# Softmax steps, products with v, pair loads and token steps moved to other points of a hand-written order

## The chip, the cores and the metric

The kernel runs on one core of one Trainium2 chip. The metric is device time in microseconds: the median of three runs of the kernel before is 1833.87 us (1829.96 to 1837.31). A profile is one more execution, with its own time.

## What is computed

Pooled attention followed by two feed-forward layers. The queries are used as they are; keys and values are averaged over groups of 8 tokens first, so each head has 72 keys.

```python
batch, n_heads, seq, head_dim = (8, 8, 576, 64)
k_p = k.reshape(B, H, Sp, pool, D).mean(axis=3)      # pool = 8, Sp = 72
v_p = v.reshape(B, H, Sp, pool, D).mean(axis=3)
scores = scale * np.matmul(q, k_p.transpose(0, 1, 3, 2))
scores = scores - np.max(scores, axis=-1, keepdims=True)
attn = np.exp(scores)
attn = attn / (np.sum(attn, axis=-1, keepdims=True) + 1e-09)
x = np.matmul(attn, v_p)                             # then (B * S, H * D) = 4608 x 512
h = x @ w_in; y = np.maximum(0.01 * h, h) @ w_out    # d_ff = 2048
xn = y / sqrt(mean(y * y) + 1e-6) * rms_g
g = xn @ w_gate; out = (g * sigmoid(g) * (xn @ w_val)) @ w_out2   # d_ff = 1536
```

All is float32. The kernel splits each operand of a product into a high and a low part and adds three products of them, so each matrix product is three matmuls (`TERMS`).

## The kernel before

Each engine works off its own queue in order: at the end the kernel ties every instruction of an engine to the one emitted before it. The order in which the program emits is therefore the order in which each engine runs, and an instruction that waits holds up what is behind it on its engine. SP issues all DMAs, also in order.

**First layer, tiles j = 0 to 4.** The 4608 tokens are nine tiles of 512. For the first five, `h_half` computes half of an h chunk (six matmuls of 512 columns) and `y_unit` half of its contribution to y (six more), two chunks of f later. After the second half of h, ScalarE applies the leaky ReLU twice (`h_high`, L101) and VectorE subtracts (`h_low`, L620). Each such piece of six matmuls is a chunk, and after each chunk `attention_point()` runs what has been put on the next point: the late attention (`late_attention`) and the conversion of weights for later (side units).

**Late attention.** Attention of batches 0 and 1 stands in the list `FIRST`. Batches 2 to 7 are 30 query tiles (five a batch), and tile i starts at point s = 33 + 8 (i - 10); `after` is the start of the next tile. `stage(kind, b, t, points)` puts one step of a generator on each of the points:

- `s` (step_s): scores of the first four heads on TensorE (sc, L322), then maximum and subtraction on VectorE (L335, L336); the same for the other four heads; the exponential on ScalarE (L341); sum, small addition, reciprocal and multiplication on VectorE (L343 to L346). Six steps.
- `r`: copies on ScalarE (er, L374), at s + 5. `t`: transposition of the next tile's queries (qt) with its copy, at s + 5.
- `x` and `y`: transpositions of the softmax (xt, L383, and xr) with their evictions to at and atr, at s + 6 and s + 7.
- `kt`: transposed pooled keys of the next batch and their copies on ScalarE (L294), at s + 3 of the fourth and fifth tile of a batch.
- `av0`, `av1`: the products with v (L426, L431) for the first two and the last three query tiles, four each (p = 0 to 3, two heads each), at points of the tile that follows, with an eviction on ScalarE (L445 or L453) and, where x stays on the chip, a subtraction on VectorE (L460). Where x goes to DRAM, SP's store is put two points later.

On one point, stages that were put by an earlier tile come first. For batches 1 to 7 the scores, kt, qt, xt, xr and the products share two banks of PSUM (tag `att`).

**First layer, pairs.** The last four tiles of tokens are two pairs, computed with seven products in place of eight (`Quad`; p1 to p7 with the names x, y, w for its sums). While the second half of pair 0's output runs as pieces of six matmuls (`queue_out`, `out_part`, each second one issuing a load of w_out by `load_o`), the loop at L1639 also issues the four loads of pair 1's tokens (`pair_loads`: xst from x in DRAM), its token steps (`token_steps`: sums, and splits into high and low parts on ScalarE, VectorE and POOL) and the splits of pair 0's own second half (`second_half`, k = 4 to 15). `tick()` runs the side units. Four pieces are left for the next pair. The loads write the slots of `up` that second_half k = 0 to 7 have read.

**Second layer.** Five pairs with a gate, a value and an output product; not touched by the change, though the loop is shared (`kinds[q] == 1` marks pairs of the first layer; only at q = 0 is the next pair of that kind too).

The functions that the change touches and what calls them:

Of the kernel before, what the change touches and what calls it, by code (L numbers as in the profile page):

```python
# [23 lines left out]
def pooled_attention_then_two_ffns(  # L24
# [14 lines left out]
    B, H, S, D = q.shape  # L39
# [431 lines left out]
    def go(kind, b, t):  # L471
        if (kind, b, t) not in running:
            running[kind, b, t] = emit[kind](b, t)
        if running[kind, b, t] is not None:
            next(running[kind, b, t], None)
# [33 lines left out]
    def late_attention():  # L509

        def put(point, f):
            at_point.setdefault(point, []).append(f)

        def stage(kind, b, t, points):
            for point in points:
                put(point, lambda: go(kind, b, t))
            if kind in use:
                def free():
                    live["q" if kind == "t" else "kv"] -= 1
                put(points[0] + 3, free)  # L520

        start = {}
        for i in range(FIRST_LATE, len(tiles) + 1):
            start[i] = 33 + 8 * (i - 10)
        for r, point in enumerate((4, 9, 14, 28, 30)):
            stage("kp", 2, r, (point,))
        stage("kt", 2, 0, (28,) * 2)
        stage("kt", 2, 1, (32,) * 2)
        stage("t", 2, 0, (28,) * 2)
        for i in range(FIRST_LATE, len(tiles)):  # L530
            b, t = tiles[i]
            s, after = start[i], start[i + 1]
            stage("s", b, t, (s, s, s + 1, s + 1, s + 3, s + 4))
            stage("r", b, t, (s + 5,))
            stage("x", b, t, (s + 6,) * 3)
            stage("y", b, t, (s + 7,) * 3)
            if i + 1 < len(tiles):
                stage("t", *tiles[i + 1], (s + 5,) * 2)
            if t < 2:
                for k in range(3):  # L540
                    stage("vp", b, 3 * t + k, (s + 2 * k,) * 2 + (s + 2 * k + 2,) * 2)
            if t in (2, 3) and b + 1 < B:
                for k in range(3 if t == 2 else 2):
                    stage("kp", b + 1, 3 * (t - 2) + k, (s + 4 * (t - 2) + 2 * k,))
                stage("kt", b + 1, t - 2, (after + 3,) * 2)
            if t in (1, 4):
                for p in range(NP):
                    stage(f"av{t // 4}", b, p, (after + 1 + p,) * 3)

    point_now = [0]  # L550
    first_left = {"V1l5", "T14c"}
# [395 lines left out]
    pairs, kinds = [], []  # L947
# [207 lines left out]
    def load_a():  # L1155
        if a_count[0] < len(a_todo):
            i = a_count[0]
            a_count[0] += 1
            if len(a_todo[i]) == 3:
                load_o_into(a_todo[i], "a", i)  # L1160
                return
            q, p, m, s = a_todo[i]
            assert {f"{m}{p}_{c}" for c in range(2)} <= ready
            t = slot("a", i, f"a{m}{q}_{p}_{s}")
            if m == "h" and s in (0, 3):
                n = 512 if s == 0 else 256
                nc.sync.dma_start(
                    out=t.rearrange("p h n -> p (h n)")[:, :2 * n].rearrange("p (h n) -> p h n", h=2).bitcast(F32),
                    in_=wi_dram[2 * p + s // 3][:, :, 512 - n:],
                )  # L1170
                a_tiles[q, p, m, s] = t.rearrange("p h n -> p (h n)")[:, :2 * n].rearrange(
                    "p (h a c n) -> p a c h n", h=2, c=2, n=P
                )
                return
            k = 2 if s < 3 else 1
            nc.sync.dma_start(
                out=t.rearrange("p h n -> p (h n)")[:, :k * 512].bitcast(F32),
                in_=op_dram[m, p][:, s, 0:k].rearrange("p a c n -> p (a c n)"),
            )
            a_tiles[q, p, m, s] = t.rearrange("p h n -> p (h n)").rearrange(  # L1180
                "p (a c h n) -> p a c h n", a=2, c=2, h=2
            )
# [143 lines left out]
    def second_half(q, k):  # L1326

        f = blocks(q, 1)[k]
        src = up[q, "f", f // 2][:, f % 2, :]
        if k % 4 != 1:  # L1330
            t = per.tile([P, 2, N], F32R, tag="ghl", bufs=3, name=f"ug{q}_{f}")
        else:
            t = p2.tile([P, 2, N], F32R, tag="ahl", bufs=1, name=f"ug{q}_{f}")
        split(nc.scalar, t[:, HI, :], nc.gpsimd if k % 2 else nc.vector, t[:, LO, :], src)
        up[q, 2, f] = t
# [186 lines left out]
    def piece():  # L1522
        if pieces:
            pieces.pop(0)()
# [16 lines left out]
    def tick():  # L1541
        for x in late_side.pop(0) if late_side else ():
            x()

    for q, (_, n) in enumerate(pairs):
        assert not late_side or kinds[q] == 1
        quads = [Quad(q, p, m) for p, m in QUADS[kinds[q]]]
        more = q + 1 < len(pairs)
        loads, xs, norm = [], None, []
        if more:  # L1550
            xs, steps = (pair_loads if kinds[q + 1] == 1 else norm_steps)(q + 1)
            if kinds[q + 1] == 1:
                loads = steps
            else:
                norm = steps
        n_norm = len(norm)

        def between():
            if norm and (i >= 2 or i == 1 and len(norm) > n_norm - 2):
                norm.pop(0)()  # L1560

        def h_quad(i, a):
            def spot():
                if norm and (i >= 3 or i >= 1 and len(norm) > n_norm - 2):
                    norm.pop(0)()
                tick()

            def out_piece():
                piece()
                spot()  # L1570

            a.p1()
            spot()
            a.p6()
            spot()
            out_piece()
            a.p2()
            load_a()
            spot()
            a.p7()  # L1580
            spot()
            out_piece()
            a.p5()
            spot()
            a.p4()
            load_a()
            spot()
            out_piece()
            a.p3()
            load_a()  # L1590
            load_a()
            spot()
            out_piece()
            if q == i == 0:
                piece()
            queue_out(q, 0, (2 * a.p, 2 * a.p + 1))

        def quad(i, a):
            for step in (a.p6, a.p5, a.p2, a.p7):
                step()  # L1600
                between()
                if step == a.p2:
                    load_a()
                    load_a()
            piece()
            if i + 1 < len(quads):
                quads[i + 1].p1()
            a.p4()
            a.p3()
            load_a()  # L1610
            load_a()

            if i + 1 < (len(quads) if more else len(quads) - 2):
                piece()
            if a.m == "v":
                queue_out(q, 0, (2 * a.p, 2 * a.p + 1))

        for i, a in enumerate(quads):
            if kinds[q] == 1:
                h_quad(i, a)  # L1620
                continue
            if i == 0:
                a.p1()
            quad(i, a)
        assert not norm
        early, late = token_steps(q + 1, xs, kinds[q] == 1) if more else ([], [])
        if kinds[q] == 1:
            second_half(q, 0)
            second_half(q, 1)
            for i in range(4):  # L1630
                piece()
                tick()
                if i > 1:
                    second_half(q, i)
        while pieces:
            piece()
        queue_out(q, 1, blocks(q, 1))

        for i in range(len(pieces) - (4 if more else 0)):  # L1639
            if kinds[q] == 1:  # L1640
                if loads and i in (6, 9, 12, 15):
                    loads.pop(0)()
                piece()
                if early + late and (i >= 16 if kinds[q + 1] == 1 else i >= 4 and i % 2 == 0):
                    (early or late).pop(0)()
                for k in (4, 5) if i == 3 else (i // 2 + 4,) if i % 2 and i > 3 else ():
                    if k < F1:
                        second_half(q, k)
                tick()
                continue  # L1650
            if i % 3 == 0 and early + late:
                (early or late).pop(0)()
            piece()
        assert not early + late
# [41 lines left out]
```

## Time and profile before

| | |
|---|---|
| median of three runs | 1833.87 us |
| profiled execution, its own time | 1832.07 us |
| span of its instructions | 1830.4 us |
| TensorE (PE) busy | 1750.5 us, 96% |
| VectorE (DVE), ScalarE (ACT), GpSimd (POOL) busy | 934.7, 718.1, 649.1 us |
| mean granted clock of TensorE | 0.988 |
| DMA | 406.36 MB, mean 222 GB/s |

The profile names instructions by line, engine, operation and tile (out<-in). PE is TensorE's matmuls, PEld its weight loads, SPq the queue of SP. "Idle before" is the time in which an engine stood idle just before an instruction, with what ended it. The granted clock is a share of full speed: 1.0 is 2.4 GHz, 0.5 is 1.2 GHz. Late attention lies between about 170 and 645 us of the span, the two pairs of the first layer between 645 and 960 us, the second layer behind them.

### The profile page before, as it was taken

The page shows a single profiled execution, that of the slowest core. Times are in us where ns is not written, and L with a number is a line of the kernel's source. Part 1 is how long each engine was busy: PE and PEld are TensorE (multiplying, and loading weights), DVE is VectorE, ACT ScalarE, POOL GpSimd, SP SyncE. Part 2 cuts the span into 40 slices and gives each one's busy share as a digit, 9 for nine tenths or more (in the row PEclk, how much of TensorE's full clock was granted, in tenths as well). Part 3 has the DMA queues.
Part 4 walks back from the last instruction along what each step waited for, and adds up shares of the span by engine and source line. Part 5 has one row for each costly group of instructions (what it writes and reads, how often), then busy time and mean ns, then how long its engine had stood idle before and what let it go on. Part 6 is the DMA issues. An engine that isn't in the chain of part 4 may idle for free.

```text
span 1830.4 us, 24096 instructions
## 1 busy us (share of the span) xinstructions
PE 1750.5 (96%) x8440; PEld 1478.9 (81%) x8440; DVE 934.7 (51%) x1633; ACT 718.1 (39%) x1527; POOL 649.1 (35%) x797
## 2 busy tenths in 40 slices
PE   5899999999998999998999999999999999999999
PEld 4789777777777788876888888899788889988887
DVE  7984445545455544465665344445534444463331
ACT  5664344434444444444554333233233323322220
POOL 5632324545243013354534432045143304513330
PEclk9899999999999999998999999999999999999999
DMA  8543554545576469987987755687765668675562
GB/s 245 197 140 125 212 192 145 164 139 179 169 226 200 145 227 335 320 329 276 344 304 225 247 182 198 218 322 252 249 240 191 203 217 311 243 274 201 196 207 92
DMA packets 214729, 406.36 MB, mean 222 GB/s; under 512 B 58704, under 2 KB 116560, under 8 KB 214096
## 3 DMA queue, kind: packets, MB, share of 16 engines
q1 hardware_dynamic: 214608, 404.82, 65.4%
q8 instruction: 67, 1.10, 0.2%
q14 instruction: 54, 0.44, 0.1%
HBM read 328.21 MB, written 76.55 MB: 221 GB/s over the span
## 4 chain that ended last, share of the span: by engine, by line
PE 80%; DVE 9%; ACT 4%; DMA 3%; issue 2%; POOL 1%; SPq 1%; ACTq 0%; POOLq 0%; DVEq 0%
PE o L1364 15%; PE h L597 9%; PE o L1344 7%; PE y L642 7%; PE yg L1236 6%; PE yv L1236 6%; PE xg L1236 4%; PE xv L1236 4%; PE wg L1236 4%; PE wv L1236 4%; PE yh L1236 3%; PE wh L1236 2%; PE xh L1236 2%; PE sc L322 2%; DMA wo<-wo 1%
## 5 line engine op out<-in xcount | busy, mean ns | idle before, releaser
L1364 PE MATMUL o<-wo,u 128*128 128x512 f32 x1296 | 316.4, 392 | 3.3 <-DMA wo<-wo 3.2
L1364 PEld LDWEIGHTS o<-wo,u 128*128 128x128 f32 x1296 | 243.3, 189 | 52.8 <-DMA wo<-wo 4.2
L597 PE MATMUL h<-xhl,w_i 128*128 128x512 f32 (+1 forms) x996 | 253.5, 396 | 6.3 <-DVE ghl L620 5.0
L597 PEld LDWEIGHTS h<-xhl,w_i 128*128 128x128 f32 x996 | 177.7, 191 | 37.3 <-DVE ghl L620 5.4
L642 PE MATMUL y<-ghl,w_o 128*128 128x256 f32 (+1 forms) x768 | 154.6, 346 | 0.0
L98 POOL TENSOR_TENSOR u<-e2g,u 128x512 fp32r<-128x512 f32 (+1 forms) x25 | 29.6, 1182 | 311.8 <-ACT u L95 311.8
L620 DVE TENSOR_TENSOR ghl<-h,ghl 128x512 fp32r<-128x512 f32 (+1 forms) x83 | 55.7, 671 | 164.3 <-ACT h L101 164.1
L642 PEld LDWEIGHTS y<-ghl,w_o 128*128 128x128 f32 x768 | 118.1, 192 | 12.8
L642 PE MATMUL y<-ghl,wr 128*128 128x512 f32 x384 | 104.2, 407 | 0.0
L1344 PE MATMUL o<-u,wo 128*128 128x512 f32 x384 | 96.2, 389 | 0.0
L1344 PE MATMUL o<-ug,wo 128*128 128x512 f32 x384 | 89.6, 390 | 0.7 <-DMA wo<-wo 0.7
L1344 PEld LDWEIGHTS o<-ug,wo 128*128 128x128 f32 x384 | 72.0, 188 | 16.9 <-issue 1.9
L1344 PEld LDWEIGHTS o<-u,wo 128*128 128x128 f32 x384 | 72.1, 188 | 15.0
L1236 PE MATMUL yg<-T,ag 128*128 128x512 f32 (+1 forms) x360 | 84.0, 368 | 0.0
L1236 PE MATMUL yv<-T,av 128*128 128x512 f32 (+1 forms) x360 | 83.8, 368 | 0.0
L1236 PE MATMUL xg<-xa,ag 128*128 128x512 f32 (+1 forms) x360 | 83.7, 367 | 0.0
L1236 PE MATMUL xv<-xa,av 128*128 128x512 f32 (+1 forms) x360 | 83.7, 367 | 0.0
L642 PEld LDWEIGHTS y<-ghl,wr 128*128 128x128 f32 x384 | 69.5, 191 | 12.3
L1236 PEld LDWEIGHTS yg<-T,ag 128*128 128x128 f32 x360 | 66.0, 188 | 10.0 <-DVE e1v L1213 0.6
L1236 PEld LDWEIGHTS yv<-T,av 128*128 128x128 f32 x360 | 66.2, 188 | 9.5
L1236 PEld LDWEIGHTS xv<-xa,av 128*128 128x128 f32 x360 | 66.1, 188 | 9.6
L1236 PEld LDWEIGHTS xg<-xa,ag 128*128 128x128 f32 x360 | 66.1, 188 | 9.4
(204 smaller groups left out, 3424.1 us busy)
## 6 DMA issues: line engine op xcount, KB each, us to landing
wo<-wo SPq DMA_DIRECT2D x172, 512.0 KB
ag<-op_g SPq DMA_DIRECT2D x90, 512.0 KB
av<-op_v SPq DMA_DIRECT2D x90, 512.0 KB
wr<-wo SPq DMA_DIRECT2D x32, 512.0 KB
ah<-op_h SPq DMA_DIRECT2D x32, 512.0 KB
k<-in_k_dram SPq DMA_DIRECT2D x40, 256.0 KB
q<-in_q_dram SPq DMA_DIRECT2D x40, 256.0 KB
op_g<-parts_g SPq DMA_DIRECT2D x36, 256.0 KB
```

Source lines behind the costliest of these rows:

```text
L98: lo_eng.tensor_tensor(out=lo, in0=src, in1=hi.bitcast(F32), op=ALU.subtract)
L322: nc.tensor.matmul(pt[:, i * n:(i + 1) * n], y[:, p, :], kblk[b % 2][:, p * n:(p + 1) * n], start=True, stop=True,)
L597: nc.tensor.matmul(pt, w[:, sp, c * P:(c + 1) * P], x[c][:, mp, c0:c1], start=c == 0 and i == 0, stop=c == KC - 1 and i == 2,)
L620: nc.vector.tensor_tensor(out=t[:, LO, :], in0=pt, in1=t[:, HI, :].bitcast(F32), op=ALU.subtract)
L642: nc.tensor.matmul(pt, w[:, sp, m * P:(m + 1) * P], g[:, mp, a - c0:a - c0 + n], start=ydone[j, a] == 1 and i == 0 and m % per_bank == 0, ...
L1236: nc.tensor.matmul(pt, wt[:, a, c, sp, :], xt[:, mp, :], start=start and c == 0 and i == 0, stop=c == 1 and i == 2, skip_group_check=not s ...
L1344: nc.tensor.matmul(pt, w[:, sp, m * P:(m + 1) * P], u[:, mp, :], start=f == blocks(q, z)[0] and i == 0, stop=f == blocks(q, z)[-1] and i == 2,
L1364: nc.tensor.matmul(pt, u[:, sp, m * P:(m + 1) * P], w[:, mp, :], start=f == 0 and i == 0, stop=f == F2 - 1 and i == 2,)
```

## The change

Three things move; no instruction is added or left out.

```diff
@@ late_attention
-            stage("s", b, t, (s, s, s + 1, s + 1, s + 3, s + 4))
+            stage("s", b, t, (s, s, s + 1, s + 1, s + 2, s + 3))
@@ late_attention
-                    stage(f"av{t // 4}", b, p, (after + 1 + p,) * 3)
+                    stage(f"av{t // 4}", b, p, (after + (2 if b + 1 < B else 1) + p,) * 3)
@@ the loop over the pieces of a pair's second half
-                if loads and i in (6, 9, 12, 15):
+                if loads and i in (4, 6, 9, 11):
                     loads.pop(0)()
                 piece()
-                if early + late and (i >= 16 if kinds[q + 1] == 1 else i >= 4 and i % 2 == 0):
+                if early + late and (i >= 13 if kinds[q + 1] == 1 else i >= 4 and i % 2 == 0):
                     (early or late).pop(0)()
```

The exponential of each of the 30 late tiles stands one point earlier, and so do the four instructions behind it. The products with v stand one point later, except those of the last batch. Between pair 0 and pair 1 of the first layer, the four loads and the ten token steps stand two to four pieces earlier.

## Rows read from the trace of the kernel before

**Rows 1.** Table of stretches: length, busy time of each engine (instructions), clock, DMA.

```profile
170.00:650.00 480.00, 447.01 (x2247) 366.22 (x2246) 247.43 (x538) 204.09 (x522) 179.64 (x318) 0.99 0.56 182
650.00:780.00 130.00, 130.00 (x577) 107.78 (x576) 61.25 (x116) 60.49 (x123) 39.56 (x50) 1.00 0.91 305
...
880.00:1830.00 950.00, 942.49 (x4367) 805.15 (x4365) 434.10 (x645) 310.75 (x557) 311.10 (x269) 1.00 0.67 233
```

**Rows 2.** Waits of PE from 170 to 650 us: total, times, longest.

```profile
PE xt L383 <- DVE ex L346: 26.0, 26, 2.9
PE sc L322 <- DVE ex L336: 4.6, 6, 2.5
PE sc L322 <- ACT xs L453: 1.4, 3, 0.5
PE xt L383 <- ACT xs L453: 0.6, 1, 0.6
```

**Rows 3.** Timeline of one late tile: start, duration, engine, line, out<-in, idle before.

```profile
225.84 0.46 DVE L336 TENSOR_TENSOR ex<-sc,st 128x288 f32<-128x288 f32 x1
...
228.23 1.41 ACT L294 COPY kblk<-kt 64x72 f32<-64x72 f32 x8 [4.36 <-PE kt L281]
...
229.66 0.69 ACT L341 ACTIVATE ex<-ex 128x576 f32<-128x576 f32 x1
...
231.48 0.69 DVE L620 TENSOR_TENSOR ghl<-h,ghl 128x512 fp32r<-128x512 f32 x1 [5.18 <-ACT h L101]
...
232.09 0.74 DVE L343 TENSOR_REDUCE st<-ex 128x8 f32<-128x576 f32 x1
...
233.70 0.85 DVE L346 TENSOR_TENSOR ex<-ex,st 128x576 f32<-128x576 f32 x1
...
234.70 0.63 PE L383 MATMUL xt<-ident,ex 128*128 128x128 f32 x4 [1.91 <-DVE ex L346]
```

**Rows 4.** Timeline before the first and third drop of the clock; the third in a table.

```profile
311.95 0.63 PE L383 MATMUL xt<-ident,ex 128*128 128x128 f32 x4 [2.28 <-DVE ex L346]
...
594.54 0.63 PE L383 MATMUL xt<-ident,ex 128*128 128x128 f32 x4 [2.89 <-DVE ex L346]
...
595.80:599.30 3.50, 3.50 (x11) 2.66 (x10) 1.52 (x3) 0.73 (x3) 0.00 (x0) 0.51 0.00 0
```

**Rows 5.** Waits of PE from 780 to 880 us.

```profile
PE xh L1236 <- ACT e1h L1279: 4.7, 1, 4.7
PE yh L1236 <- DVE e6h L1213: 2.3, 1, 2.3
...
PE o L1344 <- DMA wo<-wo: 0.7, 2, 0.4
```

**Rows 6.** Timeline: products with v and their subtractions.

```profile
207.97 0.52 PE L426 MATMUL av<-at,vb 128*128 128x256 f32 x3
...
209.06 0.42 DVE L460 TENSOR_TENSOR xhl<-av,xhl 128x256 fp32r<-128x256 f32 x1
...
216.71 0.41 DVE L460 TENSOR_TENSOR xhl<-av,xhl 128x256 fp32r<-128x256 f32 x1
```

**Rows 7.** Chain of waits at the change of pairs, then its timeline.

```profile
802.49 7.31 DMA xst<-x
...
809.92 0.69 DVE L1075 TENSOR_TENSOR T<-xst,xst 128x512 f32<-128x512 f32 x1 [2.44 <-DMA xst<-x]
...
829.54 0.56 ACT L1279 COPY e1h<-xh 128x512 f32<-128x512 f32 x1
...
835.35 2.93 PE L1236 MATMUL yh<-T,ah 128*128 128x512 f32 x6 [2.27 <-DVE e6h L1213]
```

**Rows 8.** Table of stretches at the change of pairs.

```profile
786.00:820.00 34.00, 33.27 (x145) 26.66 (x144) 19.86 (x30) 12.55 (x26) 16.91 (x15) 1.00 1.02 383
...
828.00:838.00 10.00, 5.58 (x12) 3.97 (x13) 7.82 (x11) 4.50 (x10) 7.69 (x9) 0.50 0.58 180
```

**Rows 9.** Line 98 from 780 to 850 us: times, shortest/median/longest in ns.

```profile
L98 DVE TENSOR_TENSOR ug<-u,ug x7: 685/694/1234, 780.3 to 821.9; 128x512 fp32r<-128x512 f32 x7
```

## The prediction

> **What bounds the kernel now.** I read the table of stretches first. TensorE is busy almost everywhere: from 650 to 780 us it is never idle, and from 880 us to the end it is idle 7.5 us in 950. From 170 to 650 us, where the late attention runs between the pieces of the first layer, it is busy 447.01 of 480.00 us: 33.0 us of idle time in one stretch [rows 1]. There VectorE is busy 52% and ScalarE 43% of the time, so no other engine is full; TensorE waits for the order of the work, not for its amount.
>
> Then the waits of TensorE in that stretch. 26.0 us in 26 waits are the transposition xt (L383) waiting for the last instruction of the softmax (L346); 0.6 us more is xt behind a copy of a product with v; the second scores (sc, L322) wait 4.6 us for the subtraction L336 and 1.4 us for an eviction of a product with v. Together 32.6 of the 33.0 us [rows 2].
>
> Third, the timeline of one tile, to see why the softmax is late [rows 3]. The subtraction for the second half of the heads ends at 226.30. The exponential starts at 229.66 only: it is queued on ScalarE behind the copies of kt (228.23, 1.41 us), which wait for their own transposition. The sum (L343) starts at 232.09, behind the subtraction L620 of an h chunk (231.48). The multiplication L346 ends at 234.55, and xt starts at 234.70 after 1.91 us of idle. No data was missing for 3.4 us before the exponential: it is a matter of place in two in-order queues.
>
> Fourth, the granted clock. After each of the three longest waits of this stretch (2.28 us before xt at 311.95, 2.5 us before the second scores near 367, 2.89 us before xt at 594.54) the clock falls to its lower level, 1.2 GHz, while TensorE has work. The last of the three drops is shown: 0.51 over 3.5 us in which TensorE is never idle [rows 4].
>
> Last, the change of pairs near 820 us, where xh waits 4.7 us and yh 2.3 us [rows 5].
>
> **Softmax a stage sooner.** Per late tile it moves five instructions and adds none: the exponential from point s+3 to s+2, sum, small addition, reciprocal and multiplication from s+4 to s+3. None issues a DMA; SP's and POOL's queues are not passed. On ScalarE the exponential now stands ahead of the kt copies, on VectorE the four stand ahead of L620. In the tile of [rows 3] the exponential can start at about 226.35 and end at 227.05, and the four, which took 234.55 - 232.09 = 2.46 us, can end near 229.6. TensorE would reach xt at 234.70 - 1.91 = 232.79, so 3.2 us are in hand. What is queued behind the exponential (kt copies, then the prelus of the next h chunk) waits for it only if L336 is late; L620 waits behind the four instructions, up to 2.5 us, but its result feeds a y chunk eight chunks on. In a tile with products with v the four stand behind a product's eviction and subtraction: from the product's start 1.5 us (207.97 to the end of its subtraction at 209.48 [rows 6]), then 2.5 us, 4.0 together, while TensorE still has two more products and three chunks to do before xt; a chunk is six matmuls, 6 x 130.00 / 577 = 1.35 us by the full stretch of [rows 1], and a product of four shorter ones some 0.8 us, about 5.6 us in all. The wait goes in both kinds. What remains: nothing at the least, the whole 26.6 us at the most. I take 2 us, nearest to the slack of 3.2 us, for tiles in which a side unit's VectorE work is in the way. Gain 24.6 us.
>
> **Products with v a stage later.** In ten places (the first and last group of query tiles of batches 2 to 6) the four products move from points s+1..s+4 to s+2..s+5, with their evictions, and with the stores of x that SP issues two points after each (they pass other DMAs of SP by one point; their readers come over 20 points later). Today the first product takes one of the two banks between the first and second scores, and the second scores wait for the eviction of one or the other: nine waits, 6.0 us, 2.5 us at the worst [rows 2]. With the product behind the second scores that wait has no cause. One of the nine is in the last batch, which is not moved; I leave it its 0.5 us. Gain 5.5 of 6.0 us. What is late next: the third product now stands at the point whose h chunk loads ScalarE, and the fourth directly ahead of qt and xt, so these need evictions that were further off. Today a product at the third point was off its bank only when the subtraction begun at 216.71 ended, at 217.12 [rows 6], a few tenths behind the chunk that follows it. Bounds of the new waits: 0 and, with the mean of today's nine (0.67 us) at both transpositions of ten tiles, 13 us. I take 2 us, since the eviction ends close to the time when the bank is wanted.
>
> **Clock.** Each of the three drops is 3.5 us at half speed [rows 4] and so costs 1.7 us. Without the waits ahead of them they go: gain 5.1 us, 0 if another gap stands there.
>
> **Pair loads and token steps sooner.** This part acts once, between the two pairs of the first layer. Today the fourth load of x is issued at 802.49 and lands at 809.80 (7.31 us). VectorE then starts the sums at 809.92, and from there a chain of splits and subtractions runs to e1h at 829.54, which releases xh, and to e6h, which releases yh at 835.35 [rows 7]. The clock is at 0.50 from 828 to 838 [rows 8]. The change puts the four loads at pieces 4, 6, 9, 11 for 6, 9, 12, 15 and the ten token steps at 13..22 for 16..25. On SP the loads pass loads of w_out (wo) and stores of side units. But the DMA engines are full in this stretch: share 1.02, 383 GB/s from 786 to 820 [rows 8]. So the fourth load gains what it overtakes: two wo loads of 512 KB and two stores of 256 KB by their shapes, 1.57 MB at 383 GB/s, 4.1 us. The tiles it writes are free by then, for their last readers are emitted at pieces 3 and 7. It pushes up to two wo loads back, 1.4 us each; they hold no spare time (TensorE waited for them twice, 0.7 us in all [rows 5]), but a wait there is covered by the longer one at xh. The chain starts 4.1 us sooner, with one subtraction for k=12 (0.69 us [rows 9]) newly in it: 3.4 us. To that comes the half speed after 835.35, of which I count 1.1 us. Gain 4.5 us; bounds: loss of 2.8 us (both wo loads late and the chain unmoved), gain of 12 us (all waits of this stretch, 8 us, and 4 us of the lower clock).
>
> What speaks against this part: the splits on VectorE last 0.69 us alone and up to 1.23 us in this stretch, when POOL is at work [rows 9]. The Trainium skill says why ("GPSIMD Engine Reference", Specifications): GpSimd shares its SBUF interfaces with VectorE, and an instruction with two SBUF inputs is in contention with it. By that rule the token steps, moved towards the side units' work on POOL, stretch as they move; with five more of them at the long duration the gain of this part would be 4.5 - 5 x 0.54 = 1.8 us and the time 1799.
>
> **The sum.** 24.6 + 5.5 + 5.1 - 2.0 + 4.5 = 37.7 us. The profiled execution took 1832.07 us (span 1830.4). From 650 to 780 TensorE never waits and afterwards hardly [rows 1], and every transfer and side unit there is placed by pieces of TensorE's work, not by time, so what is saved in front should reach the end. 1832.07 - 37.7 = 1794.4; the median of the runs shown, 1833.87, is 1.8 us above the profiled execution, which gives 1796.
>
> **Rivals.** (1) Half of it comes back: the freed time turns into waits of qt, xt and the products for evictions, because the two banks and the in-order queues are as tight as before. For it: the second scores already wait for ScalarE's evictions in three tiles [rows 2], and after the change there are fewer chunks between eviction and reuse. Against it: VectorE and ScalarE are half idle. With half of 33.2 us of the attention part given back: 1796 + 17 = 1813. (2) The move does little: the four instructions remain behind something else that is late (a side unit's subtraction waiting for POOL), and only the order of the scores and the transition improve: 5.5 + 1.7 + 4.5 - 2.0 = 9.7 us, 1824. Against it: in [rows 3] nothing stands between the two subtractions and the new place. (3) Slower: the exponential, now ahead of the kt copies and the prelus, blocks ScalarE whenever VectorE's L336 is late, and the prelus, the evictions of qt and xt and with them TensorE wait in every tile. It was late by 2.5 us once [rows 2]. If it costs each of the 30 tiles 1.9 us (the wait of [rows 3], now elsewhere), that is 57 us against 37.7: 1834 + 19 = 1853. It decides from 37.7 / 30 = 1.3 us a tile on. Against it: the exponential's data lay ready 3.4 us before it ran.
>
> **How the numbers follow.** My forecast 0.68, with a range of its own of 1786 to 1806; rival 1 0.16; rival 2 0.10; rival 3 0.06. Range 1784 (everything gained: 32.6 + 5.1 + 12 us, 1834 - 50) to 1818, which takes in rival 1. About 0.5%, 9 us, is what a measurement of this kernel can tell from no change. Forecast, rival 1 and half of rival 2 are faster by more: 0.89; the other half is the same: 0.05; slower 0.06.
>
> **What would show it.** In the profile after: the waits of xt for L346 under 4 us in all; the exponential ahead of the kt copies and L346 ending ahead of L620 of the same f; no wait of the second scores for L336 but in the last batch; the clock at full level from 180 us to the change of pairs; TensorE's idle time from the first late tile to the last under 6 us; the fourth load of x landing some 4 us sooner against the pieces around it, xh's wait under 2 us. New waits of qt or xt for evictions of products would show rival 1. The forecast is wrong if idle time of over 20 us remains in the attention stretch, or if the pair stage, reached 33 us sooner, waits for wo loads.

## The result, and the profile after

The changed kernel takes 1789.71 us in the median of four runs (1787.97 to 1791.39), the kernel before 1832.13 us in four, one run more than stood ahead of the prediction: a ratio of 0.9764 (of the means), with a 95% interval of 0.9739 to 0.9790. The forecast was 1796, its range 1784 to 1818. The profiled execution after took 1791.22 us (span 1789.5), 40.85 us less than the profiled one before.

To see where the time went I cut both spans at four instructions that exist once in each kernel: xt of the first late tile, xt of the last, the first o<-ug of pair 0, and the third start of xh behind it.

| Stretch | before, us | after, us | saved | forecast |
|---|---|---|---|---|
| xt of first late tile to xt of last | 452.23 | 412.49 | 39.7 | 33.2 |
| from there to the first o<-ug | 139.17 | 139.13 | 0.0 | 0 |
| first o<-ug to third xh (change of pairs) | 66.33 | 64.44 | 1.9 | 4.5 |
| from there to the end | 984.05 | 984.96 | -0.9 | 0 |

The first stretch in both kernels, as rows of the table of stretches (length; busy time with instructions of PE, PEld, DVE, ACT, POOL; clock; share of the DMA engines; GB/s). Before:

```profile
188.62:640.85 452.23, 419.99 (x2112) 343.75 (x2112) 239.49 (x522) 193.06 (x491) 172.04 (x301) 0.99 0.55 177
```

After:

```profile
188.48:600.97 412.49, 408.69 (x2112) 342.38 (x2111) 241.82 (x521) 194.69 (x489) 176.10 (x300) 1.00 0.60 193
```

Two things are to be read here. TensorE's idle time falls from 32.2 to 3.8 us. And its busy time falls too, by 11.3 us, although it runs the same 2112 matmuls. Of the 11.3 us, 5.1 are the three clock drops of [rows 4]; in the trace after, the clock is at full level throughout the stretch. The other 6.2 us had no place in my sum; they are taken up below.

What TensorE still waits for, from 155 to 610 us after (total, times, longest); it answers to [rows 2]:

```profile
PE qt L302 <- issue: 1.2, 1, 1.2
PE qt L302 <- DVE xhl L460: 1.0, 1, 1.0
PE sc L322 <- ACT xs L453: 0.5, 1, 0.5
PE sc L322 <- DVE atr L404: 0.4, 1, 0.4
PE xt L383 <- ACT xs L453: 0.3, 1, 0.3
PE qt L302 <- PE av L431: 0.2, 1, 0.2
...
```

All 26 waits of xt for L346 are gone, and so are those of sc for L336; 36 waits have become 7. The tile of [rows 3] shows why. After, on VectorE and ScalarE (start, duration, engine, line, out<-in, idle before):

```profile
223.61 0.46 DVE L336 TENSOR_TENSOR ex<-sc,st 128x288 f32<-128x288 f32 x1
...
224.16 0.69 ACT L341 ACTIVATE ex<-ex 128x576 f32<-128x576 f32 x1 [2.53 <-DVE ex L336]
...
225.99 1.41 ACT L294 COPY kblk<-kt 64x72 f32<-64x72 f32 x8 [1.15 <-PE kt L281]
226.10 0.76 DVE L346 TENSOR_TENSOR ex<-ex,st 128x576 f32<-128x576 f32 x1
...
228.55 0.69 DVE L620 TENSOR_TENSOR ghl<-h,ghl 128x512 fp32r<-128x512 f32 x1 [1.69 <-ACT h L101]
```

The exponential follows its subtraction at once and stands ahead of the kt copies. L346 ends at 226.86, ahead of L620. TensorE reaches xt at 230.38 and does not wait; 3.5 us are in hand.

The change of pairs went less well. TensorE's waits there, 735 to 840 us after, answer to [rows 5]:

```profile
PE yh L1236 <- DVE e6h L1213: 3.1, 1, 3.1
PE o L1344 <- DMA wo<-wo: 2.5, 4, 0.9
PE o L1344 <- POOL ug L98: 0.9, 1, 0.9
PE o L1344 <- DVE ug L98: 0.4, 1, 0.4
PE xh L1236 <- ACT e1h L1279: 0.3, 1, 0.3
```

The long wait of xh (4.7 us) is gone, but yh waits 3.1 us instead of 2.3, o for loads of wo 2.5 instead of 0.7, and o for splits of ug 1.3 more. Two loads there, after, from the chain of waits (start, duration):

```profile
748.87 8.15 DMA wo<-wo
757.10 9.74 DMA xst<-x
```

And VectorE's chain from its start to its end, with the group of TensorE that it releases, from the timeline:

```profile
766.92 0.69 DVE L1075 TENSOR_TENSOR T<-xst,xst 128x512 f32<-128x512 f32 x1 [4.78 <-DMA xst<-x]
...
786.71 2.38 DVE L98 TENSOR_TENSOR xb<-xst,xb 128x512 fp32r<-128x512 f32 x2
789.01 0.97 DVE L728 TENSOR_SCALAR raw_v<-raw_v 128x512 int32<-128x512 uint32 x1
...
791.16 1.58 DVE L742 TENSOR_TENSOR raw_v<-raw_v 128x128 f32<-128x128 f32 x4
792.66 0.68 DVE L1213 TENSOR_TENSOR e6h<-yh,e1h 128x512 f32<-128x512 f32 x1
793.40 2.93 PE L1236 MATMUL yh<-T,ah 128*128 128x512 f32 x6 [3.13 <-DVE e6h L1213]
```

Counted from the first o<-ug, the fourth load is issued 5.5 us sooner than in [rows 7] (22.47 before, 17.00 after), but takes 9.74 us instead of 7.31, so VectorE's sums (L1075) start 3.1 us sooner (29.90, 26.82). At the end yh is 2.0 us sooner (55.33, 53.30). Right ahead of e6h VectorE works off three conversions of weights for later, L728 to L742, from 789.01 on: 3.65 us that nothing on TensorE's path asked for. They stood there in the kernel before as well, for 2.81 us (VectorE before):

```profile
831.80 0.97 DVE L728 TENSOR_SCALAR raw_v<-raw_v 128x512 int32<-128x512 uint32 x1
...
834.61 0.68 DVE L1213 TENSOR_TENSOR e6h<-yh,e1h 128x512 f32<-128x512 f32 x1
```

### The profile page after: what moved, and what is told of

It reads as the page before. It is cut to its first block, busy times and chain, and to the rows that moved or that the text cites. A ratio compares the mean times of both kernels' runs of the same rounds, so it can differ in the third digit from the quotient of the medians.

```text
span 1789.5 us, 24094 instructions
## 1 busy us (share of the span) xinstructions
PE 1739.8 (97%) x8440; PEld 1477.3 (83%) x8440; DVE 936.5 (52%) x1633; ACT 720.3 (40%) x1527; POOL 652.2 (36%) x797
## 4 chain that ended last, share of the span: by engine, by line
PE 88%; DVE 5%; DMA 4%; ACT 1%; issue 1%; SPq 1%; POOL 1%; POOLq 0%; ACTq 0%; DVEq 0%
PE o L1364 16%; PE y L642 11%; PE h L597 10%; PE o L1344 8%; PE yg L1236 6%; PE yv L1236 6%; PE xv L1236 4%; PE xg L1236 4%; PE wv L1236 4%; PE wg L1236 4%; PE yh L1236 4%; PE wh L1236 2%; PE xh L1236 2%; PE sc L322 2%; DMA wo<-wo 2%; PE av L426 1%
## 5 line engine op out<-in xcount | busy, mean ns | idle before, releaser
L1364 PE MATMUL o<-wo,u 128*128 128x512 f32 x1296 | 316.4, 392 | 4.2 <-DMA wo<-wo 4.0
L1364 PEld LDWEIGHTS o<-wo,u 128*128 128x128 f32 x1296 | 243.1, 189 | 53.9 <-DMA wo<-wo 5.4
L620 DVE TENSOR_TENSOR ghl<-h,ghl 128x512 fp32r<-128x512 f32 (+1 forms) x83 | 55.6, 669 | 88.3 <-ACT h L101 88.2
L101 ACT ACTIVATE ghl<-h 128x512 fp32r<-128x512 f32 (+1 forms) x83 | 48.3, 582 | 65.0 <-PE h L597 63.1
```

Of the source, the lines that this page charges most:

```text
L101: return nc.scalar.activation(out=out, in_=in_, func=AF.Prelu, scale=scale, alpha=alpha)
L620: nc.vector.tensor_tensor(out=t[:, LO, :], in0=pt, in1=t[:, HI, :].bitcast(F32), op=ALU.subtract)
L1364: nc.tensor.matmul(pt, u[:, sp, m * P:(m + 1) * P], w[:, mp, :], start=f == 0 and i == 0, stop=f == F2 - 1 and i == 2,)
```

## The experiments

The theory after the result: the softmax's place carries nearly all of the attention part, and on which engine is open (VectorE, where the four instructions stood behind L620, or ScalarE, where the exponential stood behind the kt copies). The products are worth a few us. At the change of pairs the gain is small because loads of wo are pushed back and because conversions stand ahead of e6h. Each text below says what its rivals would give. In the table the median is of that kernel's runs, the ratio is to runs of the kernel before on the same chip, and the two stretches are from its profiled run.

| Kernel | median, us | ratio [95%] | late attention | change of pairs |
|---|---|---|---|---|
| before | 1832.13 | 1 | 452.23 | 66.33 |
| e1 softmax alone | 1796.93 | 0.9802 [0.9785, 0.9818] | 416.35 | 66.50 |
| e2 products alone | 1825.12 | 0.9956 [0.9944, 0.9968] | 443.08 | 67.98 |
| e3 pair loads and steps alone | 1832.12 | 0.9993 [0.9981, 1.0004] | 450.48 | 64.47 |
| e4 softmax and products | 1793.29 | 0.9781 [0.9763, 0.9799] | 412.94 | 66.72 |
| e5 exponential alone | 1825.23 | 0.9963 [0.9945, 0.9980] | 444.69 | 67.21 |
| e6 the four of VectorE alone | 1797.46 | 0.9809 [0.9794, 0.9824] | 417.45 | 66.89 |
| e7 = e4 and the loads | 1793.61 | 0.9789 [0.9772, 0.9807] | 412.78 | 65.81 |
| e8 = e4 and the steps | 1794.22 | 0.9792 [0.9777, 0.9807] | 412.78 | 68.28 |
| e0 the whole change again | 1790.73 | 0.9779 [0.9766, 0.9793] | 412.22 | 64.82 |
| e9 = e0, conversions behind e6h | 1784.84 | 0.9752 [0.9739, 0.9765] | 412.56 | 59.45 |
| e10 = e0, loads spread | 1792.78 | 0.9792 [0.9778, 0.9805] | 412.73 | 66.79 |
| e11 = e9 and e10 | 1786.37 | 0.9760 [0.9746, 0.9773] | 412.97 | 60.50 |

**The softmax alone** (e1).

```diff
-            stage("s", b, t, (s, s, s + 1, s + 1, s + 3, s + 4))
+            stage("s", b, t, (s, s, s + 1, s + 1, s + 2, s + 3))
```

> Only the softmax steps are moved (exponential to s + 2, normalisation to s + 3). Theory A: a stall of TensorE costs its idle time in the profile, plus some 0.23 us of drained pipeline that the profile counts as busy, plus 1.7 us for a drop of the clock behind it. Then the waits of xt for L346 fall from 26.0 us in 26 to under 2 us, two of the three drops go, and the attention stretch is 25 + 26 x 0.23 + 3.4 = 34 us shorter: some 1798 us against 1832. Theory B: a stall costs its idle time and the drop alone: 28 us, 1804. Rival C (the parts only work together, because products and softmax share VectorE): under 20 us, over 1812.

The late attention is 35.9 us shorter, nine tenths of what the whole change saves there. TensorE's waits from 165 to 655 us:

```profile
PE sc L322 <- DVE ex L336: 3.7, 6, 1.6
PE sc L322 <- ACT xs L453: 1.4, 3, 0.5
...
```

No wait of xt for L346 is left, and the clock stays at 1.00 in this stretch. Of the two theories on the price of a wait, A (34 us) is the near one and B (28 us) is not. The waits of the second scores stay, as the products have not moved.

**The products alone** (e2).

```diff
-                    stage(f"av{t // 4}", b, p, (after + 1 + p,) * 3)
+                    stage(f"av{t // 4}", b, p, (after + (2 if b + 1 < B else 1) + p,) * 3)
```

> Only the products with v are moved. Theory A: eight waits of the second scores go (5.5 us, 1.8 us of drained pipeline, one drop of the clock 1.7 us), but with the normalisation still at s + 4, behind the eviction of the third product, xt waits 0.5 to 1 us longer in ten tiles: 0 to 5 us faster, 1827 to 1832. Theory B: the same without the 1.8 us. Rival C (independent parts, no new waits): 9 us, 1823.

TensorE's waits from 165 to 655 us:

```profile
PE xt L383 <- DVE ex L346: 22.9, 19, 3.3
PE xt L383 <- DVE xhl L460: 1.7, 5, 0.6
PE av L426 <- DVE ex L336: 1.2, 1, 1.2
...
PE sc L322 <- ACT xs L453: 0.5, 1, 0.5
```

The waits of the second scores go as forecast (6.0 to 0.5 us), and the stretch is 9.2 us shorter, more than the 3.5 us that I gave the products and than the 0 to 5 us of theories A and B. Its idle time falls by 6.2 us in nine waits fewer; the clock drops as long as before (5.1 us). Of the new waits for which I took 2 us off, only 1.2 us of a product's wait stand here. The waits of xt change little, 26.6 to 25.2 us: in five tiles xt now waits for the fourth product's subtraction (L460), which comes behind the softmax's four, instead of L346. The two parts overlap: 35.9 + 9.2 = 45.1 alone, 39.3 together (e4). Of the 5.8 us between, 1.4 are these waits of xt, which go with the softmax in any case, and 2.4 are waits of qt that stand in e4 and in neither part alone; the rest is not followed up.

**Loads and steps of the pair alone** (e3).

```diff
-                if loads and i in (6, 9, 12, 15):
+                if loads and i in (4, 6, 9, 11):
-                if early + late and (i >= 16 if kinds[q + 1] == 1 else i >= 4 and i % 2 == 0):
+                if early + late and (i >= 13 if kinds[q + 1] == 1 else i >= 4 and i % 2 == 0):
```

> Only the pair loads and token steps are moved. From the two traces the change of pairs became 1.9 us shorter where 4.5 were forecast. Theory A: it is worth the same alone, 1.5 to 2.5 us, 1830. Rival C: alone it is worth the 4.5 us of the forecast and the attention part took some of it away (1827).

The change of pairs takes 64.47 us, as in the whole change, with the same waits (yh 3.1, wo 2.3, POOL's ug 0.9). In the median time this cannot be told from nothing: the interval takes in 1. In the late attention, which e3 leaves as it was, the clock drops twice instead of three times (450.48 us against 452.23), so a drop more or less can stand between two profiles with nothing changed there.

**Softmax and products together** (e4), the first two diffs.

> Softmax steps and products with v moved, the pair left as before. Theory A: the 39.9 us that the traces show up to the second half of pair 0 remain, and the change of pairs is as before: 1792 to 1793 us. Rival C (the parts are not additive): away from the whole change by more than 4 us.

The late attention takes 412.94 us: the whole of the gain there. At the change of pairs the old waits stand: xh 4.7, yh 2.3, wo 1.0 us. Over e1 the products bring 3.4 us, where 3.5 were forecast. TensorE's waits for qt (1.2 for "issue", 1.0 for L460) come in here; e1 has neither.

**Which engine the softmax was late on** (e5, e6).

```diff
e5: +            stage("s", b, t, (s, s, s + 1, s + 1, s + 2, s + 4))
e6: +            stage("s", b, t, (s, s, s + 1, s + 1, s + 3, s + 3))
```

> Only the exponential is moved (s + 2), the normalisation stays at s + 4. Theory V (the wait of xt is made by VectorE's order: the normalisation stands behind L620): little changes, xt still waits some 0.7 us in most tiles, 18 us in all; the drops behind the longest waits may go; 5 to 12 us faster, 1820 to 1827. Theory S (it is made by ScalarE's order: the exponential stands behind the kt copies): most of the 26 us go, over 20 us faster, under 1812.

> The exponential stays at s + 3, the normalisation moves there too and so stands ahead of L620. Theory V: nearly all of the waits of xt go, 28 to 34 us faster, 1798 to 1804; only where kt copies stand ahead of the exponential a wait of 0.1 to 0.5 us may remain. Theory S: the tiles with kt copies (the twelve fourth and fifth tiles but the last two) keep their waits, 13 us of the 26; 15 us faster, 1817.

The exponential alone brings 7.5 us of the late attention; the four on VectorE alone bring 34.8, nearly all of e1's 35.9. The timeline of the tile of [rows 3] in e5, ScalarE, VectorE and TensorE:

```profile
227.71 0.69 ACT L341 ACTIVATE ex<-ex 128x576 f32<-128x576 f32 x1 [2.53 <-DVE ex L336]
...
232.10 0.69 DVE L620 TENSOR_TENSOR ghl<-h,ghl 128x512 fp32r<-128x512 f32 x1 [4.48 <-ACT h L101]
232.71 0.74 DVE L343 TENSOR_REDUCE st<-ex 128x8 f32<-128x576 f32 x1
...
234.82 0.63 PE L383 MATMUL xt<-ident,ex 128*128 128x128 f32 x4 [0.73 <-DVE ex L346]
```

The exponential ends at 228.40, and VectorE stands idle for 4.48 us, with the sum's data there from 228.40 on: L620 is ahead of the sum in the queue and waits for ScalarE's prelu. In e6 it is the other way round (ScalarE, VectorE and TensorE):

```profile
226.59 1.42 ACT L294 COPY kblk<-kt 64x72 f32<-64x72 f32 x8 [4.36 <-PE kt L281]
228.03 0.69 ACT L341 ACTIVATE ex<-ex 128x576 f32<-128x576 f32 x1
...
228.74 0.75 DVE L343 TENSOR_REDUCE st<-ex 128x8 f32<-128x576 f32 x1 [4.08 <-ACT ex L341]
...
229.97 0.86 DVE L346 TENSOR_TENSOR ex<-ex,st 128x576 f32<-128x576 f32 x1
230.75 0.68 DVE L620 TENSOR_TENSOR ghl<-h,ghl 128x512 fp32r<-128x512 f32 x1
...
230.98 0.63 PE L383 MATMUL xt<-ident,ex 128*128 128x128 f32 x4
```

The exponential still waits for the kt copies, but the four stand ahead of L620 and are done at 230.83, and xt at 230.98 doesn't wait. So the order on VectorE set the time; ScalarE's place was late, but not what decided.

**The pair part taken apart** (e7: the loads at 4, 6, 9, 11 with the old steps; e8: the steps from 13 on with the old loads; both with softmax and products).

> Softmax and products moved; at the change of pairs the loads at pieces 4, 6, 9, 11, the token steps at 16 to 25 as before. Theory L (the landing of the fourth load sets the start of the sums): the sums start with the load, which no longer ends last; the steps at piece 18 start near 805 on the old time base, 2 to 3 us sooner, and the time is within 1 us of the whole change. Theory T (the piece at which the steps are emitted decides): no gain over the kernel with softmax and products alone.

> Softmax and products moved; at the change of pairs the token steps at pieces 13 to 22, the loads at 6, 9, 12, 15 as before. Theory L: the sums at piece 15 wait for the fourth load, which is no sooner, and VectorE and ScalarE stand still behind them, splits of the second half among them: no gain or a loss of 1 to 3 us against softmax and products alone, with waits of o for the splits ug. Theory T: most of the 1.9 us.

Neither alone brings the gain. The loads alone give 65.81 us at the change of pairs, the steps alone 68.28, e4 66.72, both 64.82. The six kernels with the old places for loads and steps lie between 66.33 and 67.98 there, with a mean of 66.9, so e7's difference is hardly more than their spread and e8 is 0.3 us beyond it; the waits show the mechanism better. In e7 the sums wait for no load, but at their old place in the order they start only 0.8 us sooner than in e4 (29.03 us behind the first o<-ug, 29.87). In e8 VectorE waits for the fourth load, and TensorE for what is queued behind that (VectorE and TensorE):

```profile
769.74 0.69 DVE L1075 TENSOR_TENSOR T<-xst,xst 128x512 f32<-128x512 f32 x1 [7.88 <-DMA xst<-x]
...
776.49 1.74 DVE L98 TENSOR_TENSOR ug<-u,ug 128x512 fp32r<-128x512 f32 x1
...
778.29 4.61 PE L1344 MATMUL o<-ug,wo 128*128 128x512 f32 x12 [3.04 <-DVE ug L98]
```

A step that is emitted before its load has landed holds up pair 0's own split of ug, and that costs 3.0 us of TensorE.

**The whole change again, and two edits on it** (e0, e9 to e11, one chip). e9 holds three calls of the side units back until e6h has been emitted, and makes up for them two at a time; e10 issues the four loads at pieces 0, 2, 6 and 10. In the diff of e9 lines are left out and the remarks behind # are added.

```diff
e9, against the changed kernel:
-    def tick():
-        for x in late_side.pop(0) if late_side else ():
-            x()
+    owed = [0]
+    def tick(held=False):
+        if held:
+            owed[0] += 1
+            return
+        for _ in range(2 if owed[0] else 1):
+            for x in late_side.pop(0) if late_side else ():
+                x()
+        owed[0] = max(owed[0] - 1, 0)
...
-                tick()                                 # in spot()
+                tick(q == 1 and i == 0 and not a.sixth)   # a.sixth: set behind p6
...
-                tick()                                 # in the loop over the pieces
+                tick(more and kinds[q + 1] == 1 and i >= 26)
e10, against the changed kernel:
-                if loads and i in (4, 6, 9, 11):
+                if loads and i in (0, 2, 6, 10):
```

> The whole change once more, beside the three kernels that follow: 1788 to 1792 us.

> The whole change, and three ticks of the side units (pieces 26 and 27 and the first spot of pair 1) are held back until e6h is emitted, so that L728, L732 and L742 no longer stand ahead of it on VectorE. Theory K (after the change these conversions, 3.6 us on VectorE and waiting for ScalarE, end last before yh): yh's wait of 3.1 us falls under 0.5 us, no drop of the clock behind it, 3 to 5 us faster than the whole change. Theory P (the chain of splits itself ends last): yh's wait stays over 2 us, under 1 us gained.

> The whole change with the pair loads at pieces 0, 2, 6, 10 for 4, 6, 9, 11. Theory Q (the engines of the DMA are full from piece 4 on, so a load is sooner only where it is issued before): the four waits of o for wo, 2.5 us, fall under 1.2 us and the sums start 1 us or more sooner; 1 to 2 us faster. Theory R (the order of wo and xst loads makes no difference, all of it is late): waits for wo stay over 2 us and the time is unchanged, or the first loads hold up wo loads at pieces 2 and 3 and new waits of 1 us stand there.

> Conversions held back and loads at pieces 0, 2, 6, 10. By K and Q together 4 to 6 us faster than the whole change, 1784 to 1786; by P and R unchanged.

e0 repeats the result: 1790.73 us, the late attention within 0.3 us and the change of pairs within 0.4 of the profile after. e9 beats both kernels: 1784.84 us (1783.94 to 1788.07) against 1790.73 (1787.90 to 1792.69) for e0 on the same chip, 5.9 us less, and 5.4 us of that at the change of pairs. The timeline of VectorE and TensorE there in e9:

```profile
786.41 2.39 DVE L98 TENSOR_TENSOR xb<-xst,xb 128x512 fp32r<-128x512 f32 x2
788.73 0.68 DVE L1213 TENSOR_TENSOR e6h<-yh,e1h 128x512 f32<-128x512 f32 x1
789.33 0.41 DVE L728 TENSOR_SCALAR raw_v<-raw_v 128x512 int32<-128x512 uint32 x1
...
789.46 1.66 PE L1236 MATMUL yh<-T,ah 128*128 128x512 f32 x6
```

TensorE's waits in e9 from 735 to 840 us:

```profile
PE o L1344 <- DMA wo<-wo: 1.4, 2, 0.8
PE o L1344 <- POOL ug L98: 0.9, 1, 0.9
PE o L1344 <- ACT ug L95: 0.9, 1, 0.9
...
```

e6h is the next instruction behind the splits, 3.7 us sooner than after (counted from the first o<-ug: 48.82, 52.56), and yh doesn't wait. The clock, 0.57 from 793 to 797 us after, is at 1.00 from 785 to 800 here. Counted from the first o<-ug, yh starts 3.8 us sooner (49.55, after 53.30), and from there to the third xh it is 9.90 us instead of 11.14, as no drop follows: 5.0 us against the profile after, 5.4 against that of e0. That the conversions were what e6h stood behind is shown. As they stand there in the kernel before too, this gain is not one that the change opened; e9's edit on the kernel before was not run.

e10 gave the other of the two readings that its text weighs. The sums start hardly sooner (26.6 us behind the first o<-ug, after 26.8, e0 27.1), and the wo loads that the early x loads pass are late in one piece (TensorE's waits in e10 from 735 to 840 us):

```profile
PE o L1344 <- DMA wo<-wo: 3.5, 1, 3.5
PE yh L1236 <- DVE e6h L1213: 3.1, 1, 3.1
```

e11 has both and is no better than e9: its wo wait is 3.7 us, its change of pairs 60.50. So x loads put still further ahead bring the sums half a microsecond at most, and the change of pairs is 1 to 2 us longer with them (66.79 against 64.82, 60.50 against 59.45).

## Why the prediction was right, and where it was not

**What bounds.** Right. The order of the work and not its amount held TensorE: with no instruction taken out, TensorE's idle time in the late attention went from 32.2 to 3.8 us.

**Softmax, 24.6 us of idle.** Right in mechanism and near in size: all 26.0 us of the waits for L346 went, none of the 2 us that I left. But e5 and e6 show that one of the two queues would have been enough; in my reading of [rows 3] the exponential behind the kt copies came first and L620 second. It was L620.

**Products, 5.5 - 2.0 us.** Right: 3.4 us over the softmax alone, of which 2.4 are idle time, the kind that I had added up. The waits of sc fell from 6.0 to 0.9 us, and new ones came for qt (1.2, 1.0 and 0.2 us), about the 2 us that I took.

**Clock, 5.1 us.** Right: no drop is left from 170 to 610 us, and none in this stretch in any kernel that has the four of VectorE moved.

**What the sum lacked.** Idle time and clock add up to 28.4 + 5.1 = 33.5 us of the 39.7 saved. The 6.2 us that remain are in TensorE's busy time. They come from the ends of the matmuls in front of each wait. The group ahead of xt in the tile of [rows 3], before:

```profile
231.14 1.64 PE L642 MATMUL y<-ghl,w_o 128*128 128x512 f32 x6
```

The same group after, and the xt behind it:

```profile
228.91 1.64 PE L642 MATMUL y<-ghl,w_o 128*128 128x512 f32 x6
230.38 0.60 PE L383 MATMUL xt<-ident,ex 128*128 128x128 f32 x4
```

After, xt starts 1.47 us behind the start of y, while y is still shown as running. Before, it started 234.70 - 231.14 = 3.56 us behind. The wait cost 2.09 us, and the profile shows 1.91 us of idle. So a wait costs about 0.2 us more than its idle time: 6.2 / (36 - 7) = 0.21 us each. With that one figure, idle time and drops (5.1 us where all three go) the other kernels come out: e1 loses 25 waits and 25.5 us of idle, and 25.5 + 25 x 0.21 + 5.1 = 35.9 (measured 35.9); e6 loses 23 and 24.7, 34.6 (34.8); e4 29 and 27.9, 39.1 (39.3). e2 and e5, where clock drops remain, fit worse (8.1 for 9.2, 7.8 for 7.5). The Trainium skill ("Perfetto Trace Analysis", Identifying the Most-Contended Engine) says that the busy time of matmuls is not a good measure of how close a kernel is to its roofline, because pipelined instructions look smaller in the trace. The trace agrees: beside the clock's 5.1 us, the same 2112 matmuls show 6.2 us less where fewer waits part them.

**Pair loads and token steps, 4.5 us.** The step that failed. Measured 1.9 us by the landmarks (2.4 us as the means of three kernels against six), and nothing that the median of e3 can tell. Three terms of 4.1 - 0.7 + 1.1 were off; the profiles give 3.1 - 1.1 - 0.1. The sums start 3.1 us sooner instead of 4.1, since the fourth load's own transfer grew from 7.31 to 9.74 us. From the sums to e6h it takes 25.74 us instead of 24.69, 1.05 us longer where 0.69 was reckoned; 0.84 us of that are the three conversions (2.81 to 3.65), since I followed the chain to e6h without asking what else stands in VectorE's queue ahead of it. And the 1.1 us of half speed did not come back: yh still waits, the clock is low behind that wait in both kernels (0.50 from 828 to 838 us before, 0.57 from 793 to 797 after), and from yh to the third xh it is 11.00 us before and 11.14 after. The six kernels with the old places spread from 11.0 to 12.5 us there, the three with the change have 11.1 to 11.2, so in the mean about half of this term may stand.

The waits of o for wo did grow, from 0.7 to 2.5 us, which the prediction named as a sign of being wrong. They come from the order of the loads and not from reaching the pair sooner: e3, with the attention as before, has 2.3 us, and e4, with the pair as before, 1.0. But they cost nothing in this profile, as a longer wait still covers them, now that of yh: between the sums and e6h VectorE stands idle for ScalarE alone (1.6 us), never for TensorE. They are, with the waits for ug, why the wait of xh nearly went: TensorE reaches xh 2.7 us later, and xh itself starts only 1.6 us sooner (50.14, 48.51).

The estimate by the Trainium skill's rule on the interfaces that GpSimd and VectorE share ("GPSIMD Engine Reference", Specifications), 1.8 us for this part, is near the 1.9 measured. The trace agrees that VectorE's instructions stretch beside POOL (splits of xb last 0.68 to 1.78 us after). But the nearness is luck: the estimate took 2.7 us more off for longer splits, and the whole chain to e6h grew by 0.4 us more than was reckoned.

**The rest.** The waits of o (L1364) for wo behind the change of pairs grew from 3.2 to 4.0 us, about the 0.9 us given back. The kernels' times for this stretch scatter from 982.65 to 987.00 us, so nothing is to be read from it.

**Sum.** 37.7 forecast, 40.9 measured: +6.2 for the waits' hidden part, +0.3 of idle, -2.6 at the change of pairs, -0.9 behind it, and 0.2 elsewhere. The total is the nearer because the misses on both sides partly cancel. None of the rivals came: what took the place of the waits in the late attention is 3.8 us of idle time (rival 1 would have left 17 us), and the exponential ahead of the prelus held nothing up.

## What to carry to other kernels

Where an engine works off its queue in order, read what stands directly ahead of the late instruction on each engine of its chain, and test each engine by itself: here the order on one of two engines was worth 34.8 of 35.9 us. A drop of the clock that follows a wait is not won by moving the wait forward: here it went only where the wait went (e9). And when a chain has been shortened at its start, look for unrelated work in the queue just ahead of its end; it cost 5.4 us here and nothing in the profile's totals showed it.

## What the runs showed of the hardware that I had not expected

A wait of TensorE costs about 0.2 us more than the idle time that is shown for it, since the tail of the last matmul ahead of it counts as busy (0.18 us in the tile above, 0.21 us in the mean of 29 waits). And the fourth load of x took 9.74 us after, against 7.31 before. From its issue to the sums it is 9.5 to 9.8 us in the four kernels that issue it 17.0 to 17.5 us behind the first o<-ug and whose sums wait for it (after, e0, e3, e9), and 7.4 us in the seven that issue it 21.9 to 23.2 us behind. Why is not shown: the DMA engines are full in both kernels (a share of 0.99 and 360 GB/s from 743 to 767 us after, 1.02 and 383 in [rows 8]), and the load of wo just ahead of it took 8.15 us after and 8.04 before.
